# A second factor for GpSimd's softmax scalings, and plain copies where the factor is already in

## The chip, the cores and the metric

The kernel runs on one core of a Trainium2 chip. A core has five engines with instruction queues of their own, each worked off in order: TensorE (PE in the profile, its weight loads PEld) for matrix products and transposes, VectorE (DVE), ScalarE (ACT), GpSimd (POOL), and SyncE (SP), which here only issues DMAs. They wait for one another through semaphores. The metric is the device time of one execution in microseconds; before the change the median of three runs was 1030.27 us (1029.30 to 1031.94).

## The reference

Three stages follow one another, on float32 data. With B = 4 batches, H = 8 heads, S = 576 positions and D = 64:

```python
scores = q @ k.T / sqrt(D);  scores[causal] = -1e9
a = exp(scores - scores.max(-1));  a /= a.sum(-1) + 1e-9
local = a @ v
qp = phi(q)                                  # max(x, 0) + exp(min(x, 0))
mem_out = (qp @ M_prev) / (qp @ z_prev + 1e-6)
g = 1 / (1 + exp(-beta))                     # one gate per head
x = g * mem_out + (1 - g) * local            # 2304 tokens x 512
x = (h - tanh(h)) @ w_out,  h = x @ w_in     # first MoE layer, 512 -> 2048 -> 512
out = P(h) / (Q(h) + 1e-6) @ w2_out,  h = x @ w2_in   # second layer, a rational gate
```

So every row of the softmax is multiplied by two numbers before its product with v: one over its sum, which differs from row to row, and 1 - g, which is one number per head.

## The kernel before

Attention works on 16 head pairs n (4 batches x 4 pairs, two heads e = 0, 1 each). A head's 576 queries are cut into four rows of tiles i = 0 to 3 of 128 queries, which see (i + 1) x 128 keys, and a short tile i = 4 of 64 queries; the short tiles of both heads lie one above the other in one tile of 128 partitions, `p4`. For each (i, e): `scores` (TensorE) puts q k into a PSUM bank, `least` (VectorE) adds the mask and finds the extreme, `expo` (ScalarE) takes the exponential into the SBUF tile `p` with its row sums, `recip` (VectorE) makes one over the sum in `sm`, and `scale` (L919) multiplies `p` by it. Then `turn` (L941, TensorE) transposes `p` in blocks of 128 into a PSUM bank, `turned` (L956, ScalarE) copies the bank to the SBUF tile `pT`, and `values` (TensorE) forms the product with v. Each `p` tag has two buffers (`N_P`), `pT` has six.

Which engine scales is in `SCALES`, read at 2i + e: P is GpSimd, A is ScalarE, V is VectorE. That gives (0,0) P, (0,1) A, (1,0) V, (1,1) P, (2,0) P, (2,1) A, (3,0) P, (3,1) P and the short tile P; only for the first pair does VectorE scale (3,0). The gate factor 1 - g lies in the tile `omg`, one column for each head, made in `setup2`. It enters at one of two places. For rows 1 and the short tile it is the second factor of `scale` (L926, L929). For rows in `LATE` (0, 2, 3) `scale` multiplies by one over the sum alone (L931 on ScalarE, L933 on GpSimd or VectorE), and the copy in `turned` multiplies by `omg` (L966); the other copies are plain (L970). A copy empties a bank that holds one entry of `TURNS`: (2,0) with (0,0); (2,1) with (0,1); (3,0); (3,1); (1,0) with (1,1); and two for the short tile.

The order of all this is written out by hand: the tables `AT` and `OVER` give every step of every pair a virtual time (100 for a pair), and a heap issues the steps in that order, so that several pairs are in flight. From a virtual time of 842 on, `bg.tick` puts steps of the decoding of the first layer's weights between them (ScalarE L587 and L610, VectorE L589 to L598, GpSimd L612). Two chains of matrix products follow attention, with weights split into a high and a low part, in a fixed order too.

Of the kernel before, what the change touches and what calls it, by code (L numbers as in the profile page):

```python
# [10 lines left out]
F32 = mybir.dt.float32  # L11
# [4 lines left out]
ALU = mybir.AluOpType  # L16
# [3 lines left out]
P = 128  # L20
# [12 lines left out]
MIX = False  # L33
PSUM_DECODE = True
SCALES = "PAVPPAPPP"
LATE = (0, 2, 3)
LOW_ATT, LOW_POST, LOW_X = "P", "P", "P"
AGE_A, AGE_B, AGE_C = 1, 3, 4
EVERY = 3
TICKS_1 = (2, 2, 2, 3, 2, 3, 2, 2, 2, 2, 2, 0)  # L40
# [437 lines left out]
def kernel(  # L478
# [21 lines left out]
    nc = tc.nc  # L500
# [220 lines left out]
    class Attention:  # L721
# [197 lines left out]
        def scale(self, n, i, e):  # L919
            v, h = self.u[n, i], 2 * (n % NP)  # L920
            pt, r = v["p"][e], v["sm"][:, 6 + e:7 + e]
            how = "V" if (n, i, e) == (0, NQ - 1, 0) else SCALES[2 * i + e]
            eng = nc.vector if how == "V" else nc.gpsimd
            if i == NQ:
                og = self.cp["omg4"][:, n % NP:n % NP + 1]
                eng.tensor_scalar(pt[:, 0:S], pt[:, 0:S], r, og, ALU.mult, ALU.mult)  # L926
            elif i not in LATE:
                og = self.cp["omg"][:, h + e:h + e + 1]
                eng.tensor_scalar(pt, pt, r, og, ALU.mult, ALU.mult)  # L929
            elif how == "A":  # L930
                nc.scalar.activation(pt, pt, AF.Copy, scale=r)  # L931
            else:
                eng.tensor_scalar(pt, pt, r, None, ALU.mult)  # L933

        def busy(self, ps, count):

# [19 lines left out]
        def turned(self, n, k):  # L956
            ps = self.pair[n].pop(("tp", k))
            w = sum(nb for _, _, nb in TURNS[k])
            if w == 1:
                t = self.sp.tile([P, 1, P], F32, tag="pT5", name=f"pT{n}_{k}")  # L960
            else:
                t = self.sp.tile([P, NQ, P], F32, tag="pT", name=f"pT{n}_{k}", bufs=N_PT)
            dst, (i, e, _) = t[:, 0:w, :].rearrange("r t c -> r (t c)"), TURNS[k][0]
            if i in LATE:
                c = 2 * (n % NP) + e
                nc.scalar.activation(  # L966
                    dst, ps[:, 0:w * P], AF.Copy, scale=self.cp["omg"][:, c:c + 1]
                )
            else:
                nc.scalar.copy(dst, ps[:, 0:w * P])  # L970
            c = 0
            for i, e, nb in TURNS[k]:
                self.u[n, i].setdefault("pT", {})[e] = t[:, c:c + nb]
                c += nb
# [73 lines left out]
        def start(self, setup):  # L1048

            self.load_k(-1)  # L1050
            setup()
            self.load("qn", 0, [P, NQ + 1, P], qn, 2)
            self.load_v(0)
            self.load_z(0)
            self.load_tails()
# [216 lines left out]
    cpool = att.enter_context(tc.tile_pool(name="ac", bufs=1, side="right"))  # L1272
    sp = att.enter_context(tc.tile_pool(name="as", bufs=2, side="right"))
    cp = {}
# [3 lines left out]
    cp["g"] = cpool.tile([P, H], F32, tag="gg", name="gg")  # L1278
    cp["omg"] = cpool.tile([P, H], F32, tag="omg", name="omg")
    cp["omg4"] = cpool.tile([P, NP], F32, tag="omg4", name="omg4")  # L1280
    cp["g4"] = cpool.tile([P, NP], F32, tag="g4", name="g4")
    cp["sm"] = [cpool.tile([P, 8], F32, tag=f"sm{j}", name=f"sm{j}") for j in range(2 * NQ + 2)]
    cp["rq"] = [cpool.tile([P, S + TAIL], F32, tag=f"rq{j}", name=f"rq{j}") for j in range(2)]
# [7 lines left out]
    def setup():  # L1291
        attn.load_q(-1)
        nc.vector.memset(cp["idle"], 0.0)
        attn.busy(bT("idle"), IDLE)
        for t in cp["rq"]:
            nc.vector.memset(t[0:D, TAIL:P], 0.0)
            nc.vector.memset(t[D:P, 0:TAIL], 0.0)
        nc.gpsimd.memset(cp["mask"], 0.0)
        nc.gpsimd.affine_select(
            out=cp["mask"][:, TB:TB + P], in_=cp["mask"][:, TB:TB + P],  # L1300
            compare_op=ALU.is_ge, fill=NEG, base=0, pattern=[[-1, P]],
            channel_multiplier=1,
        )
        make_identity(nc, cp["ident"])
        for e in range(2):
            r = slice(e * TAIL, (e + 1) * TAIL)
            nc.vector.tensor_copy(cp["mask4"][r], cp["mask"][0:TAIL, TB:TB + TAIL])
        for m in cp["mb"]:
            nc.vector.memset(m, 0.0)
        nc.vector.memset(cp["p4"][:, S:S + TAIL], 0.0)  # L1310
        for sm in cp["sm"]:
            nc.vector.memset(sm, 1e-9)
        for pz in cp["pz"]:
            nc.vector.memset(pz[:, :, :, D:D + 1], 1e-6)

# [16 lines left out]
    one = Moe1(xs_a, range(NT // TA), TA, FA, wka, bHa, bYa, False, nc.vector)  # L1332
# [31 lines left out]
    for f in FB[len(FB) - KEEP:]:  # L1364
        bg.add(1, f, w_keep)
    attn.start(setup)
    calls, events = attn.events(), []
    rows = range(B * NP)
# [21 lines left out]
    while events:  # L1390
        at, _, name, n = heapq.heappop(events)
# [211 lines left out]
```

## Time and profile before

| | |
|---|---|
| median of three runs | 1030.27 us |
| the profiled execution | 1033.54 us |
| its span, first to last instruction | 1031.4 us |
| TensorE, VectorE, ScalarE, GpSimd busy in the span | 98%, 75%, 70%, 36% |
| mean granted TensorE clock | 0.992 of full speed |
| attention | about 7 to 212 us |
| first MoE layer | about 212 to 622 us |
| second MoE layer | about 622 to 1031 us |

The shares are means over stages of different kinds. In slices of a fortieth of the span, ScalarE is busy nine tenths or more in most of the first eight (attention) and seven tenths or less in the ten from the eleventh on, and GpSimd is busy eight to nine tenths in several of the first eight and a few tenths after them. Matrix products are pipelined, and the profile models their ends. Records on one engine overlap by up to 0.1 us, so that durations read one by one add up to slightly more than the time they fill.

### The profile page before, as it was taken

The numbers are of one execution on the slowest core, as the hardware profiler recorded it, in microseconds if no ns is written. First come the engines' busy times: TensorE is split into PE (matmuls) and PEld (weight loads), VectorE is DVE, ScalarE is ACT, GpSimd is POOL, SyncE is SP. The second block draws the span as 40 slices with busy tenths as digits, with TensorE's granted clock in tenths as the row PEclk, the third lists the DMA queues.
The fourth block names the chain that finished last, engine by engine and source line by source line (L and its number), as shares of the span: only waits on it lengthen the run. The fifth ranks groups of instructions, "written<-read, shape, count | busy, mean of one in ns | idle before, by whom it ended". The sixth has DMA issues, their size and how long they took to land.

```text
span 1031.4 us, 17897 instructions
## 1 busy us (share of the span) xinstructions
PE 1006.1 (98%) x6446; PEld 910.5 (88%) x6446; DVE 775.1 (75%) x1755; ACT 720.3 (70%) x1524; POOL 370.0 (36%) x338
## 2 busy tenths in 40 slices
PE   7989999989999999999999999999999999999998
PEld 4767766779998999999999998999999999999997
DVE  6768899878887367676665657987887877877885
ACT  5979999946765333333333547988888888888886
POOL 3878899924553010000000102342332423324221
PEclk8999999999999999999999999999999999999999
DMA  4434555243332125353534241000000000000000
GB/s 116 120 111 116 186 155 154 94 115 119 117 103 82 42 69 153 116 154 92 153 99 146 97 135 36 21 1 32 1 11 21 1 31 1 1 31 1 25 7 31
DMA packets 36376, 79.81 MB, mean 77 GB/s; under 512 B 8384, under 2 KB 10944, under 8 KB 36288
## 3 DMA queue, kind: packets, MB, share of 16 engines
q1 hardware_dynamic: 35824, 78.40, 25.1%
q8 instruction: 51, 0.84, 0.3%
q10 hardware_dynamic: 464, 0.27, 0.1%
q14 instruction: 37, 0.30, 0.1%
HBM read 64.49 MB, written 14.16 MB: 76 GB/s over the span
## 4 chain that ended last, share of the span: by engine, by line
PE 85%; DVE 6%; POOL 5%; ACT 2%; issue 1%; DMA 0%; ACTq 0%; POOLq 0%; DVEq 0%
PE h L1081 37%; PE y L1211 19%; PE y L1128 19%; PE pv L1006 3%; POOL p L933 2%; PE s L876 2%; PE tp L950 2%; DVE p L892 2%; PE pv L990 1%; POOL p L929 1%; POOL p L926 1%; ACT p L905 1%; DVE x L1265 1%; PE pw L1006 0%; PE php L838 0%
## 5 line engine op out<-in xcount | busy, mean ns | idle before, releaser
L1081 PE MATMUL h<-xs,w 128*128 128x384 f32 (+1 forms) x2448 | 436.4, 327 | 1.0 <-DVE g L1193 0.6
L1081 PEld LDWEIGHTS h<-xs,w 128*128 128x128 f32 x2448 | 409.6, 189 | 10.3 <-DVE g L1193 1.1
L1128 PE MATMUL y<-gh,w 128*128 128x384 f32 (+1 forms) x864 | 215.9, 318 | 2.1 <-ACT gh L1116 2.1
L1211 PE MATMUL y<-w,gh 128*128 128x512 f32 x576 | 179.6, 393 | 0.0
L1128 PEld LDWEIGHTS y<-gh,w 128*128 128x128 f32 x864 | 152.7, 189 | 2.6 <-ACT gh L1116 2.3
L1073 POOL TENSOR_TENSOR xs<-x,xs 128x256 fp32r<-128x256 f32 (+1 forms) x56 | 46.1, 849 | 274.0 <-ACT xs L1072 250.6
L1128 PE MATMUL y<-gl,w 128*128 128x384 f32 (+1 forms) x432 | 137.8, 319 | 3.4 <-DVE gl L1117 3.2
L1110 ACT ACTIVATE g<-h 128x384 f32<-128x384 f32 (+1 forms) x108 | 49.2, 455 | 127.9 <-PE h L1081 122.0
L1111 DVE TENSOR_TENSOR g<-h,g 128x384 f32<-128x384 f32 (+1 forms) x108 | 55.2, 511 | 91.8 <-ACT g L1110 91.6
L1211 PEld LDWEIGHTS y<-w,gh 128*128 128x128 f32 x576 | 106.8, 188 | 17.4
L1211 PE MATMUL y<-w,gl 128*128 128x512 f32 x288 | 114.0, 396 | 0.2
L1200 POOL TENSOR_TENSOR gl<-g,gh 128x384 fp32r<-128x384 f32 x48 | 49.5, 1031 | 150.2 <-ACT gh L1198 150.2
L1200 POOL TENSOR_TENSOR gl<-vG,gh 128x384 fp32r<-128x384 f32 x47 | 50.2, 1068 | 130.9 <-ACT gh L1198 128.7
L1116 ACT CAST gh<-g 128x384 fp32r<-128x384 f32 (+1 forms) x108 | 51.3, 475 | 62.6 <-PE y L1128 60.0
L905 ACT ACTIVATE p<-p,sm 128x128 f32<-128x128 f32 (+4 forms) x144 | 84.1, 590 | 7.7 <-DVE sm L892 6.6
L933 POOL TENSOR_SCALAR p<-p,sm 128x512 f32<-128x512 f32 (+2 forms) x63 | 80.2, 1282 | 20.1 <-DVE gg L1319 11.8
L1187 DVE TENSOR_TENSOR vA<-vA,vC 128x384 f32<-128x384 f32 x96 | 53.5, 557 | 43.0 <-ACT vC L1181 43.0
L1128 PEld LDWEIGHTS y<-gl,w 128*128 128x128 f32 x432 | 81.8, 189 | 4.1 <-DVE gl L1117 4.0
L1117 DVE TENSOR_TENSOR gl<-g,gh 128x384 fp32r<-128x384 f32 (+1 forms) x108 | 63.2, 585 | 29.5 <-ACT gh L1116 29.5
L892 DVE CUSTOM_DVE_ANT_0 p<-s,mask 128x512 f32<-128x512 f32 (+4 forms) x160 | 69.5, 477 | 14.4 <-PE s L876 13.1
L1176 DVE SCALAR_TENSOR_TENSOR vA<-vA,vC 128x384 f32<-128x384 f32 x96 | 59.1, 616 | 25.3 <-ACT vC L1175 20.2
L1180 ACT ACTIVATE vA<-h 128x384 f32<-128x384 f32 x96 | 46.9, 489 | 39.4 <-PE h L1081 37.4
(110 smaller groups left out, 1685.7 us busy)
## 6 DMA issues: line engine op xcount, KB each, us to landing
wraw<-in_w_in_dram SPq DMA_DIRECT2D x32, 512.0 KB, 4.0
wraw<-in_w_out_dram SPq DMA_DIRECT2D x32, 512.0 KB, 4.0
wk<-wf SPq DMA_DIRECT2D x36, 256.0 KB, 4.3
wx<-wk SPq DMA_DIRECT2D x18, 512.0 KB, 3.3
qn<-in_qn_dram SPq DMA_DIRECT2D x16, 320.0 KB, 3.8
vn<-in_vn_dram SPq DMA_DIRECT2D x16, 320.0 KB, 3.3
out_dram<-o SPq DMA_DIRECT2D x18, 256.0 KB, 2.0
rk<-in_kd_dram SPq DMA_DIRECT2D x30, 144.0 KB, 2.9
```

The costliest lines, as they stand in the source:

```text
L892: nc.vector.tensor_tensor_reduce(out=v["p"][-1][:, k0:k1], in0=bank[:, c0:c0 + k1 - k0], in1=mask, scale=-0.125, scalar=3.0e38, op0=ALU.ad ...
L905: nc.scalar.activation(pt, pt, AF.Exp, bias=sm[:, c:c + 1], scale=-1.0, accum_out=sm[:, 2 * e:2 * e + 1],)
L933: eng.tensor_scalar(pt, pt, r, None, ALU.mult)
L1081: nc.tensor.matmul(ps[:, 0:T], wi_of(layer, f, wp, k), xs[k][:, xp], start=(n == 0), stop=(n == 3 * NK - 1),)
L1111: nc.vector.tensor_tensor(v["g"], v["h"], v["g"], ALU.subtract)
L1116: nc.scalar.copy(v["gh"], v["g"])
L1117: self.lo.tensor_tensor(v["gl"], v["g"], v["gh"].bitcast(F32), ALU.subtract)
L1128: nc.tensor.matmul(ps, wo_of(1, f, w)[:, m * P:(m + 1) * P], v[g], start=(first and j == 0 and m % n == 0), stop=(last and j == 2), skip_g ...
L1176: nc.vector.scalar_tensor_tensor(A, A, QEPS, C, ALU.add, ALU.mult)
L1187: nc.vector.tensor_tensor(n["A"], n["A"], n["C"], ALU.mult)
L1200: eng.tensor_tensor(o["gl"], o["G"], o["gh"].bitcast(F32), ALU.subtract)
L1211: nc.tensor.matmul(acc_of[t][m], g[:, c], wo_of(2, f, w), start=(first and j == 0), stop=(last and j == 2),)
```

## The change

`LATE` now holds pairs (i, e), and only the two that ScalarE scales: (0,1) and (2,1). In `scale`, GpSimd and VectorE always multiply by two factors in one instruction, one over the sum and the gate factor; for an (i, e) in `LATE` that they would scale the second factor would be a column of ones, `one`, a new tile that set-up fills. In `turned`, the copy multiplies by the gate factor only if the first entry of the bank is in `LATE`. The tables of the order stay as they are.

```diff
-LATE = (0, 2, 3)
+LATE = ((0, 1), (2, 1))
...
             if i == NQ:
                 og = self.cp["omg4"][:, n % NP:n % NP + 1]
                 eng.tensor_scalar(pt[:, 0:S], pt[:, 0:S], r, og, ALU.mult, ALU.mult)
-            elif i not in LATE:
-                og = self.cp["omg"][:, h + e:h + e + 1]
-                eng.tensor_scalar(pt, pt, r, og, ALU.mult, ALU.mult)
             elif how == "A":
                 nc.scalar.activation(pt, pt, AF.Copy, scale=r)
             else:
-                eng.tensor_scalar(pt, pt, r, None, ALU.mult)
+                og = self.cp["one"] if (i, e) in LATE else self.cp["omg"][:, h + e:h + e + 1]
+                eng.tensor_scalar(pt, pt, r, og, ALU.mult, ALU.mult)
...
-            if i in LATE:
+            if (i, e) in LATE:
                 c = 2 * (n % NP) + e
...
+    cp["one"] = cpool.tile([P, 1], F32, tag="one", name="one")
...
+        nc.vector.memset(cp["one"], 1.0)
```

## Rows read from the trace of the kernel before

**Rows 1.** The page, part 1: busy us (share of the span) xinstructions

```profile
PE 1006.1 (98%) x6446; PEld 910.5 (88%) x6446; DVE 775.1 (75%) x1755; ACT 720.3 (70%) x1524; POOL 370.0 (36%) x338
```

**Rows 2.** Windows; columns as in the first line

```profile
core 0: us, PE busy (x) PEld busy (x) DVE busy (x) ACT busy (x) POOL busy (x), PEclk, DMA share, GB/s
91.50:102.77 11.27, 11.27 (x116) 8.51 (x118) 9.12 (x39) 10.83 (x31) 9.73 (x9) 1.00 0.41 119
114.04:125.77 11.73, 11.70 (x117) 8.54 (x118) 10.99 (x41) 11.73 (x34) 8.67 (x9) 1.00 0.30 91
150.77:163.10 12.33, 11.49 (x116) 8.48 (x118) 11.45 (x45) 12.05 (x33) 12.33 (x10) 1.00 0.52 158
125.77:199.58 73.81, 67.88 (x678) 50.25 (x680) 68.65 (x247) 72.19 (x193) 73.81 (x55) 1.00 0.47 142
440.00:624.00 184.00, 184.00 (x1063) 184.00 (x1062) 117.93 (x207) 75.85 (x151) 16.58 (x16) 1.00 0.42 125
```

**Rows 3.** Chain of waits, 150 to 163 us: start us, us, what

```profile
156.05 2.07 POOL p L933 x2
158.12 1.35 POOL p L926
159.47 1.63 POOL p L929
```

**Rows 4.** TensorE in order of time: start, us, instruction [idle before <-releaser]

```profile
53.14 0.76 PE L950 MATMUL tp<-ident,p 128*128 128x128 f32 x5 [0.95 <-POOL p L933]
54.68 0.65 PE L950 MATMUL tp<-ident,p 128*128 128x128 f32 x4 [0.78 <-POOL p L933]
...
71.42 0.66 PE L950 MATMUL tp<-ident,p 128*128 128x128 f32 x4 [0.89 <-POOL p L933]
```

**Rows 5.** Windows after the stall at 53 to 55 us (columns of rows 2)

```profile
55.00:57.00 2.00, 2.00 (x8) 0.54 (x5) 0.83 (x1) 0.44 (x1) 1.67 (x2) 0.59 0.30 88
57.00:59.00 2.00, 2.00 (x22) 1.79 (x21) 1.76 (x7) 0.00 (x0) 1.26 (x1) 0.56 0.00 0
```

**Rows 6.** GpSimd in order of time, both forms of the scaling, undisturbed

```profile
46.07 0.55 POOL L929 TENSOR_SCALAR p<-p,sm,omg 128x256 f32<-128x256 f32 x1
47.95 0.82 POOL L926 TENSOR_SCALAR p<-p,sm,omg 128x576 f32<-128x576 f32 x1 [1.33 <-DVE sm L914]
...
69.80 1.57 POOL L933 TENSOR_SCALAR p<-p,sm 128x512 f32<-128x512 f32 x1
...
72.56 0.61 POOL L933 TENSOR_SCALAR p<-p,sm 128x128 f32<-128x128 f32 x1
74.35 1.25 POOL L933 TENSOR_SCALAR p<-p,sm 128x384 f32<-128x384 f32 x1 [1.18 <-DVE sm L914]
```

**Rows 7.** GpSimd's groups by shape, 140 to 200 us: busy us, mean ns

```profile
L929 POOL TENSOR_SCALAR p<-p,sm,omg 128x256 f32<-128x256 f32 x5 | 7.5, 1498 | 0.0
...
L926 POOL TENSOR_SCALAR p<-p,sm,omg 128x576 f32<-128x576 f32 x5 | 6.9, 1388 | 0.0
```

**Rows 8.** ScalarE's groups by shape, whole span

```profile
L966 ACT ACTIVATE pT<-tp,omg 128x512 f32<-128x512 f32 x64 | 42.4, 690 | 7.9 <-PE tp L950 4.2 <-PE pv L1006 3.7
L970 ACT COPY pT<-tp 128x512 f32<-128x512 f32 x32 | 18.6, 584 | 1.1 <-PE tp L950 1.0
```

**Rows 9.** VectorE and GpSimd in order of time, first pair

```profile
14.18 0.45 DVE L1321 TENSOR_SCALAR omg<-gg 128x8 f32<-128x8 f32 x1
...
14.02 1.24 POOL L933 TENSOR_SCALAR p<-p,sm 128x384 f32<-128x384 f32 x1 [11.79 <-DVE gg L1319]
18.07 0.70 POOL L929 TENSOR_SCALAR p<-p,sm,omg 128x256 f32<-128x256 f32 x1 [2.80 <-DVE sm L917]
```

**Rows 10.** VectorE in order of time, a pair that GpSimd bounds

```profile
158.19 0.67 DVE L594 SCALAR_TENSOR_TENSOR wf<-wraw,wf 128x512 uint32<-128x512 uint32 x1
158.89 1.12 DVE L598 SCALAR_TENSOR_TENSOR wf<-wraw,wf 128x512 uint32<-128x512 uint32 x1
159.93 0.81 DVE L807 SCALAR_TENSOR_TENSOR phi<-qn,phi 128x640 f32<-128x640 f32 x1
```

**Rows 11.** GpSimd's groups by shape, 20 to 80 us

```profile
L929 POOL TENSOR_SCALAR p<-p,sm,omg 128x256 f32<-128x256 f32 x4 | 2.3, 577 | 0.0
```

## The prediction

> **What bounds the kernel now.** I read the busy table first: TensorE is busy 1006.1 of 1031.4 us and GpSimd only 370.0 [rows 1], so an edit of GpSimd looks worthless until the span is cut into stages. From about 232 us on, the kernel is matrix products almost back to back; from 440 to 624 us TensorE is busy all of 184.00 us [rows 2]. Nothing that this change touches runs there, so whatever attention (the first 210 us) gains should be carried to the end.
>
> The second view is a table of windows, cut where the value products of successive head pairs begin [rows 2]. Three kinds of pair are seen. At 91 to 103 us a pair takes 11.27 us, and TensorE is busy for all of it. At 114 to 126 us, where weight decoding joins in, it takes 11.73 us, and ScalarE is busy for all of it. In the six pairs from 125.77 to 199.58 us GpSimd is busy for all of 73.81 us; the one shown takes 12.33 us, of which TensorE works 11.49 and ScalarE 12.05. So GpSimd is the bound of six pairs, by 0.3 us a pair over ScalarE and 0.8 us over TensorE.
>
> Third, the chain of waits inside that pair [rows 3]: two one-factor scalings, the two-factor scaling of the short tile, then the two-factor one of row 1 on GpSimd, for which TensorE waits. Fourth, TensorE's waits before 80 us [rows 4]: transposes wait for one-factor scalings at 53.14 (0.95 us), 54.68 (0.78) and 71.42 (0.89). [...]
>
> **The change, part by part.**
>
> *GpSimd's scalings.* By the code each of the 16 pairs has four one-factor scalings on GpSimd (two of 512 columns, one of 384, one of 128) but for one that the first pair gives to VectorE: 63. Each gets a second factor. Undisturbed, one-factor rows last 1.57, 1.25 and 0.61 us for 512, 384 and 128 columns, and two-factor rows 0.82 us for 576 and 0.55 us for 256 [rows 6]: the form with more work is the shorter one. Two-factor is a line of (0.82 - 0.55) / (576 - 256) = 0.84 ns a column plus 0.33 us; one-factor one of (1.57 - 0.61) / 384 = 2.5 ns plus 0.29 us. By the first line the changed scalings would last 0.77, 0.66 and 0.44 us, an estimate, since these widths have no two-factor row: a pair's four fall from 2 x 1.57 + 1.25 + 0.61 = 5.0 us to 2 x 0.77 + 0.66 + 0.44 = 2.6 us. The other end: in the bound pairs the two-factor rows are stretched to means of 1.39 us (576) and 1.50 us (256) [rows 7], by 0.57 and 0.95 us. All four stretched by 0.95 us would make 6.4 us, dearer than now. I take 2.6 to 3.6 us, nearest the undisturbed rows, because what stretches them is limited (first rival). Even 3.6 us takes GpSimd's pair from 12.33 to 10.9 us, below the other two engines.
>
> [...]
>
> *ScalarE's copies.* Of a pair's four scaled 512-column copies, three become plain. Scaled they last 690 ns, plain 584 [rows 8]: 0.11 us each, 0.32 us a pair. The fourth keeps its factor, since ScalarE still does the one-factor scalings (0,1) and (2,1). The new tile of ones is read by nobody, because every pair in LATE is scaled by ScalarE, ahead of that branch; its memset is one small VectorE instruction among the set-up's, before the first scores are there: nothing.
>
> *The new wait.* In the first pair the scaling at 14.02 us must now wait for the gate factor, ready at 14.18 + 0.45 us [rows 9]. Behind it on GpSimd is the row-1 scaling, which starts only at 18.07 us after 2.80 us of idle: a delay of some 0.8 us, less 0.6 us of shortening, is hidden. Without that cover it would cost 0.2 us once. In later pairs the factor has long been there. VectorE's one changed instruction keeps its engine and width and is taken at nothing. No DMA and no queue order changes.
>
> **The sum.** Before 80 us the waits at 53, 55 and 71 us go, 0.95 + 0.78 + 0.89 = 2.6 us: the two 512-column scalings ahead of each last transpose are together 1.6 us shorter. ScalarE does not take over there; it works 0.44 of the 4 us after the stall [rows 5]. With the double stall gone the clock should stay up: 2 x 0.41 + 2 x 0.44 = 1.7 us [rows 5]; a pair that leaves TensorE idle for 12.33 - 11.49 = 0.84 us still has a clock of 1.00 [rows 2], so a small rest would not lower it. Small gains before 50 us: 0.2. Together 4.5 us, with ends 1.7 (one stall left, clock falling as before) and 5.2.
>
> From 114 to 200 us ScalarE is late next. Its work is 11.73 + 72.19 = 83.9 us [rows 2], less 7 x 0.32 = 81.7; with TensorE's 11.70 in the first of the seven windows 82.0. They last 11.73 + 73.81 = 85.5 us now. Closed up entirely, 3.5 us are gained; I leave 0.1 us of idle in each of five pairs: 3.0. Ends: 1.5 (a pair's 0.3 us of ScalarE idle stays) and 3.8.
>
> From 91 to 114 us nothing, since TensorE is full. Last pair and hand-over to the first MoE layer: 0.2, the three cheaper copies.
>
> 4.5 + 3.0 + 0.2 = 7.7 us. The profiled execution took 1033.54 us (span 1031.4), 3.3 us above the median of the runs, 1030.27; so 1025.8 by it, and 1022.6 us as the runs are timed.
>
> **Rivals.**
>
> *Contention makes it slower.* The short, dense two-factor form could be the one that collides with VectorE: the row-1 scaling lasts 1.63 us in the bound pair [rows 3] against 0.55 alone, and beside it one of VectorE's weight steps lasts 1.12 us, where its twin before it took 0.67 [rows 10]. If each of the four new ones caught that 1.08 us, they would hold 2.6 + 4.3 = 6.9 us instead of the bound pair's 2 x 1.57 + 2.07 = 5.2; 12.33 would become 14.0, and six pairs would cost 10 us: with nothing gained earlier, about 1040. It decides at 0.65 us of stretch each. Against it: before 80 us the row-1 scaling has a mean of 577 ns [rows 11]; and in the bound pair the partners are VectorE's three instructions that read two tiles, 0.67 + 0.67 + 0.81 = 2.2 us undisturbed, of which 0.54 + 1.08 = 1.6 us already fall on the two existing two-factor scalings.
>
> [...]
>
> *The form does not matter.* If the slow rows are slow for another reason (their buffers, what runs beside them), GpSimd keeps its time, only ScalarE's 0.32 us a pair is saved, and ScalarE is off the bound in six pairs of seven: 0 to 0.7 us, about 1029.8. Against it: the rows of each form lie on a line in columns, and row 1's buffers are of the same pool as the others'.
>
> *GpSimd gains, but the next wait eats part.* TensorE, ScalarE and VectorE in their fixed orders hold one another: the bound pairs fall only to about 12.1 us, 1.3 us in all, and before 80 us the stalls go but the clock still falls. 2.6 + 1.3 = 3.9 us, 1026.4. For it: ScalarE already works 98% of those pairs [rows 2].
>
> **How the numbers follow.** Forecast, 1020.3 to 1025.5: 0.62. The next wait eats part, 1025 to 1028: 0.24. The form does not matter: 0.09. Contention: 0.05. With the scatter of the runs (1029.30 to 1031.94) the range is 1019.0 to 1027.8. A measurement of this kernel can tell 0.3%, 3.1 us, from no change. The first two cases are faster by more than that, but for a corner of the second (0.02): faster 0.84, within 0.3% 0.11, slower 0.05.
>
> **What would show it.** 512-column scalings near 0.8 us in the early pairs; TensorE without the waits at 53, 55 and 71 us, and a clock of 1.0 after them; 11.8 to 11.9 us for the pairs that took 12.33, with ScalarE full in place of GpSimd; plain copies at 0.58 us. The prediction is wrong if the changed 512-column scalings stay above 1.4 us, if those pairs stay at 12.3 us, or if the stages after 232 us change their length.

## The result, and the profile after

The median fell from 1030.72 us (4 runs) to 1020.25 us (4 runs, 1019.75 to 1020.97): 10.5 us, a ratio of 0.9899 with a 95% interval of 0.9882 to 0.9917. Forecast were 7.7 us less and 1022.6 us, with a range of 1019.0 to 1027.8; the time lies near the lower end of the range, at the very edge of the first case (1020.3 to 1025.5). The profiled execution took 1020.13 us, its span is 1017.9 us. It is 13.4 us below that of before, more than the medians are apart; a likely reason is told further down.

GpSimd's scalings as groups over the whole span, of which [rows 6] showed single instructions. L931 is now the line of all but the short tile's. Columns: busy us, mean ns | idle before and releaser.

```profile
L931 POOL TENSOR_SCALAR p<-p,sm,omg 128x512 f32<-128x512 f32 x31 | 23.9, 779 | 9.4 <-DVE sm L917 9.2 <-DVE x L1263 0.2
L926 POOL TENSOR_SCALAR p<-p,sm,omg 128x576 f32<-128x576 f32 x16 | 13.9, 870 | 3.9 <-PE php L838 2.2 <-DVE sm L914 1.7
L931 POOL TENSOR_SCALAR p<-p,sm,omg 128x384 f32<-128x384 f32 x16 | 11.1, 696 | 22.4 <-ACT p L905 13.7 <-DVE sm L914 6.0 <-ACT pT L968 1.8
L931 POOL TENSOR_SCALAR p<-p,sm,omg 128x256 f32<-128x256 f32 x16 | 10.3, 642 | 3.7 <-DVE sm L917 3.7
L931 POOL TENSOR_SCALAR p<-p,sm,omg 128x128 f32<-128x128 f32 x16 | 8.5, 531 | 0.5 <-DVE sm L914 0.5
```

512 columns now take half of the 1.57 us of [rows 6], near the 0.77 of the estimate; 384 columns, at 696 ns, are close to their 0.66, and 128 columns, at 531 ns, lie a fifth above their 0.44. The two scalings that were not edited shrank too, from 1154 to 870 ns (576 columns) and from 1054 to 642 ns (256) as means of all 16.

The windows that answer to [rows 2], and one over 50 to 59 us for [rows 5]; the columns are in the first line, here and for the windows of all experiments below:

```profile
core 0: us, PE busy (x) PEld busy (x) DVE busy (x) ACT busy (x) POOL busy (x), PEclk, DMA share, GB/s
85.29:96.56 11.27, 11.27 (x116) 8.52 (x118) 8.87 (x39) 10.63 (x31) 6.80 (x9) 1.00 0.38 118
142.33:153.87 11.54, 11.49 (x116) 8.50 (x118) 10.97 (x43) 11.54 (x34) 8.02 (x10) 1.00 0.54 161
119.24:187.99 68.75, 68.28 (x679) 50.34 (x680) 65.74 (x244) 68.75 (x193) 49.50 (x54) 1.00 0.50 149
440.00:624.00 184.00, 183.97 (x1058) 183.31 (x1058) 118.45 (x208) 79.47 (x155) 17.93 (x17) 1.00 0.38 115
...
50.00:59.00 9.00, 9.00 (x94) 6.50 (x94) 7.78 (x33) 8.66 (x26) 6.04 (x7) 1.00 0.40 113
```

The six pairs that GpSimd bounded take 68.75 us instead of 73.81. One takes 11.54 us; ScalarE is busy for all of it, GpSimd for 8.02. Pairs that TensorE bounds still take 11.27 us. From 50 to 59 us TensorE does not idle and the clock is 1.00.

TensorE's waits from 20 to 200 us (us in total, times, longest), in the kernel before and then after the change. Before, ten were for a scaling: four for one with one factor (three of them in [rows 4]) and six for row 1 in the bound pairs. None is left.

```profile
PE tp L950 <- POOL p L929: 5.9, 6, 1.4
PE tp L950 <- POOL p L933: 3.3, 4, 0.9
```
```profile
PE pw L988 <- DVE x L1263: 0.9, 1, 0.9
PE s L876 <- DVE sm L892: 0.2, 1, 0.2
PE php L838 <- ACT pT L968: 0.2, 1, 0.2
```

GpSimd in the pair at 142 us, and VectorE's three two-tile instructions after it, as in [rows 3] and [rows 10]:

```profile
147.68 0.82 POOL L926 TENSOR_SCALAR p<-p,sm,omg 128x576 f32<-128x576 f32 x1
148.48 0.72 POOL L931 TENSOR_SCALAR p<-p,sm,omg 128x256 f32<-128x256 f32 x1
```
```profile
149.72 0.68 DVE L594 SCALAR_TENSOR_TENSOR wf<-wraw,wf 128x512 uint32<-128x512 uint32 x1
150.44 0.69 DVE L598 SCALAR_TENSOR_TENSOR wf<-wraw,wf 128x512 uint32<-128x512 uint32 x1
151.05 0.82 DVE L807 SCALAR_TENSOR_TENSOR phi<-qn,phi 128x640 f32<-128x640 f32 x1
```

Before, these two scalings ran at the same time as VectorE's three and lasted 1.35 and 1.63 us; now GpSimd reaches them earlier, is done at 149.2 us, and the three start at 149.72.

### The profile page after: what moved, and what is told of

Read it like the earlier page. It is cut to its first block, busy times and chain, and to the rows that moved or that the text cites. A ratio compares the mean times of both kernels' runs of the same rounds, so it can differ in the third digit from the quotient of the medians.

```text
span 1017.9 us, 17898 instructions
## 1 busy us (share of the span) xinstructions
PE 1002.1 (98%) x6446; PEld 908.7 (89%) x6446; DVE 770.3 (76%) x1756; ACT 714.6 (70%) x1524; POOL 321.2 (32%) x338
## 4 chain that ended last, share of the span: by engine, by line
PE 88%; ACT 8%; DVE 3%; issue 1%; DMA 0%; POOL 0%; ACTq 0%; DVEq 0%
PE h L1079 38%; PE y L1209 19%; PE y L1126 19%; PE s L876 4%; ACT p L905 3%; PE tp L948 3%; PE pv L1004 2%; ACT pT L968 2%; PE pv L988 1%; PE pw L1004 1%; PE php L838 1%; DVE p L892 1%; ACT p L928 0%; ACT phiT L845 0%; ACT wf L587 0%
## 5 line engine op out<-in xcount | busy, mean ns | idle before, releaser
L905 ACT ACTIVATE p<-p,sm 128x128 f32<-128x128 f32 (+4 forms) x144 | 87.5, 623 | 6.9 <-DVE sm L892 5.8
L876 PE MATMUL s<-rk,rq 64*128 64x384 f32 (+5 forms) x320 | 67.3, 467 | 3.1 <-DMA rq<-in_qd_dram 2.6
```

The costliest lines, as they stand in the source:

```text
L876: nc.tensor.matmul(bank[:, c0:c0 + k1 - k0], d["rq"][r, q0:q0 + P], d["rk"][r, k0:k1], start=True, stop=True, skip_group_check=True,)
L905: nc.scalar.activation(pt, pt, AF.Exp, bias=sm[:, c:c + 1], scale=-1.0, accum_out=sm[:, 2 * e:2 * e + 1],)
```

## The experiments

Each time is a median of several runs, beside runs of the kernel before on the same chip, unless it says otherwise; a ratio is to the kernel before. The edits shown are made to the changed kernel, but for that of the plain copies alone, which is made to the kernel before.

**The form alone.** The second factor is the column of ones, the copies keep the gate factor.

```diff
-LATE = ((0, 1), (2, 1))
+LATE = ((0, 0), (0, 1), (2, 0), (2, 1), (3, 0), (3, 1))
```

> Two factors in all of GpSimd's scalings, the second one a column of ones; the four ScalarE copies of a pair keep their gate factor as before. Theory (the form of GpSimd's scalings carries the gain): the pairs that took 12.33 us fall to 11.54 + 0.32 = 11.86 us at most, so about 8 of the 10.5 us are kept: 1022 to 1023.5 us. Rival (ScalarE's cheaper copies carry it, since ScalarE is full after the change): at most half is kept, 1025.5 us or more.

1023.08 us, ratio 0.9921 (0.9908 to 0.9934). The multiplication by one changes no value, and it brings nearly four fifths of the gain. A window over one of the bound pairs:

```profile
142.87:154.69 11.82, 11.68 (x116) 8.50 (x118) 11.06 (x43) 11.82 (x35) 8.12 (x10) 1.00 0.54 165
```

**The plain copies alone.**

```diff
-            if i in LATE:
+            if (i, e) in ((0, 1), (2, 1)):
```

> Three of the four ScalarE copies of a pair are plain, GpSimd's scalings keep one factor; the gate factor of rows (0,0), (2,0), (3,0) and (3,1) is left out of the computation. Theory (form of GpSimd's scalings): GpSimd still bounds six pairs at 12.3 us, so 0 to 1 us is gained: 1029.7 to 1030.7 us. Rival (ScalarE's copies): 5 us or more, 1025.5 us or less.

1031.24 us, against 1031.13 for the kernel before in the same runs, ratio 1.0001 (0.9990 to 1.0012): nothing. In the windows of its trace GpSimd's pair is 12.33 us as before, while ScalarE's busy time fell from 12.05 to 11.76:

```profile
149.15:161.48 12.33, 11.49 (x116) 8.49 (x118) 11.45 (x45) 11.76 (x33) 12.33 (x10) 1.00 0.51 153
54.00:58.00 4.00, 3.24 (x38) 2.32 (x40) 2.11 (x8) 1.91 (x5) 3.25 (x4) 1.00 0.44 117
```

The second line matters for the clock. In this execution TensorE's two waits near 53 us are there nearly as in [rows 4] (0.76 and 0.77 us for 0.95 and 0.78), and the clock is 1.00 after them, where [rows 5] had 0.59 and 0.56.

**Only the 512-column scalings.** As the form alone, but rows 0 and 2 keep one factor.

```diff
+                if i in (0, 2):
+                    eng.tensor_scalar(pt, pt, r, None, ALU.mult)
+                else:
+                    eng.tensor_scalar(pt, pt, r, og, ALU.mult, ALU.mult)
```

> As the run with ones, but the second factor only in the two 512-column scalings of a pair; those of 384 and 128 columns keep one factor. Theory (GpSimd only has to fall below ScalarE): GpSimd's pair falls by 1.6 us to about 10.7, below ScalarE's 11.86, and the early waits were behind 512-column scalings, so the time is within 1.5 us of the run with ones: 1022 to 1025 us. Rival (every us of GpSimd counts, by its latency in the chain): only 3.2 of GpSimd's 5.2 us are treated, so about 60% of the gain of the run with ones: 1025 to 1027 us.

1024.63 us, ratio 0.9936 (0.9923 to 0.9948), 1.55 us above the form alone, against 1.5 as the theory's limit and 2 to 4 for the rival: inside the theory's 1022 to 1025 us, if barely. A bound pair takes 11.81 us (window below) with GpSimd busy for 9.53: there the remaining one-factor scalings, 1273 and 767 ns on average, cost nothing. From the third pair on, the pairs are as long as with ones throughout. What the trace shows as lost is early and small: the value products of the third pair begin at 54.6 us instead of 52.6, and the distance stays 2.0 us from there on, but 1.2 of these were there before any scaling, since VectorE's first score came at 9.66 instead of 8.45 us. Where the rest of the 1.55 us between the medians comes from is not shown.

```profile
144.93:156.74 11.81, 11.67 (x116) 8.52 (x118) 11.44 (x43) 11.81 (x34) 9.53 (x10) 1.00 0.51 159
```

**An immediate as the second factor** (one run). `LATE` is that of the form alone.

```diff
-                og = self.cp["one"] if (i, e) in LATE else ...
+                og = 1.0 if (i, e) in LATE else ...
```

> The run with ones, but the second factor of GpSimd's 512-, 384- and 128-column scalings is an immediate 1.0 in place of a column. Theory (a second operation selects the fast form, whatever feeds it): 512 columns stay at about 0.77 us, time about 1023 us. Rival (it takes a second operand from a column to be fast): 512 columns take 1.5 us as with one factor, and the time is about 1030 us.

1023.79 us, and GpSimd's groups over the whole span:

```profile
L931 POOL TENSOR_SCALAR p<-p,sm 128x512 f32<-128x512 f32 x31 | 21.5, 704 | 10.2 <-DVE sm L917 7.0 <-ACT pT L964 2.7 <-DVE x L1263 0.5
...
L931 POOL TENSOR_SCALAR p<-p,sm 128x384 f32<-128x384 f32 x16 | 9.9, 622 | 26.8 <-DVE sm L914 14.8 <-DVE gg L1319 12.0
L931 POOL TENSOR_SCALAR p<-p,sm 128x128 f32<-128x128 f32 x16 | 6.7, 418 | 0.6 <-DVE sm L914 0.6
```

No second column is read, and 512 columns take 704 ns, against 1574 with one factor in the kernel before and 770 with the column of ones (means of 31 each). In these traces two operations took less time than one, with a column or an immediate as the second factor.

**ScalarE's two scalings moved to GpSimd as well.**

```diff
-SCALES = "PAVPPAPPP"
-LATE = ((0, 1), (2, 1))
+SCALES = "PPVPPPPPP"
+LATE = ()
```

> The change, and besides the one-factor scalings (0,1) and (2,1) move from ScalarE to GpSimd with two factors, so that all copies are plain. Theory (after the change ScalarE is the bound of seven pairs, GpSimd has 3.5 us a pair to spare, TensorE's floor is 11.27): ScalarE loses about 0.9 us a pair, GpSimd gains 1.1, the pairs fall from 11.54 to 11.27 to 11.4 us: 1 to 2 us faster than the change, 1018 to 1019.5 us. Rival (TensorE and VectorE in their order hold the pair at 11.54 already, ScalarE only looks full): no gain, 1020.3 us, or a loss where GpSimd gets in VectorE's way.

1025.59 us, ratio 0.9945 (0.9933 to 0.9958): 5 us slower than the change. The theory missed; the rival's last clause, a loss where GpSimd gets in VectorE's way, is what came in the pairs from 122 us on. These took 12.00 us, and no engine is full in them; the chain of waits runs through VectorE from 113 us on. Here are GpSimd and VectorE in order of time, and the window of that pair:

```profile
149.57 1.27 POOL L828 TENSOR_TENSOR phi<-phi,nrm 128x640 f32<-128x640 f32 x1
150.81 0.69 POOL L931 TENSOR_SCALAR p<-p,sm,omg 128x128 f32<-128x128 f32 x1
```
```profile
149.94 1.24 DVE L799 TENSOR_SCALAR phi<-qn 128x640 f32<-128x640 f32 x1
```
```profile
146.12:158.12 12.00, 11.53 (x116) 8.54 (x118) 11.68 (x45) 11.07 (x31) 9.60 (x12) 1.00 0.51 150
```

VectorE's L799, which follows the masking of row 1, lasts 1.24 us here; its median is 0.49 us in the kernel before and 0.50 in the change. It starts 0.37 us into GpSimd's L828 and ends 0.3 us after that is through (149.94 + 1.24 = 151.18 against 150.84). The added 384-column scaling, 0.67 us long, stands ahead of L828 on GpSimd and pushed it onto L799; in the change's pair at 142 us L828 is through at 144.57 + 1.26 = 145.83 and L799 starts at 146.02. In the kernel before the order was the other one: L799 began 0.11 us ahead of L828 and kept its 0.49 us, while L828 lasted 1.50 us, against 1.27 above:

```profile
166.79 0.49 DVE L799 TENSOR_SCALAR phi<-qn 128x640 f32<-128x640 f32 x1
```
```profile
166.90 1.50 POOL L828 TENSOR_TENSOR phi<-phi,nrm 128x640 f32<-128x640 f32 x1
```

In both the instruction that started second lasted longer than it does elsewhere. What held it is in no row.

This is about half of the loss. From VectorE's first score to the value products of the eighth pair the run took 101.6 us against 98.8 in the change, so 2.8 us were gone before any L799 lasted this long: there TensorE waits for GpSimd itself, 0.65 us for a scaling at 41.85 us and 1.17 us for L828 at 59.91.

**ScalarE's two scalings left out.** GpSimd's and VectorE's work as in the change.

```diff
-                nc.scalar.activation(pt, pt, AF.Copy, scale=r)
+                pass
...
-            if (i, e) in LATE:
+            if False:
```

> The change, with ScalarE's scalings of (0,1) and (2,1) left out and their copies plain, so both factors of those two rows are missing from the computation; GpSimd and VectorE do what they do in the change. ScalarE loses about 0.9 us a pair. Theory (after the change ScalarE bounds the pair of 11.54 us; moving these scalings to GpSimd failed because GpSimd then blocked VectorE): TensorE becomes the bound, 11.27 to 11.35 us a pair, 1.3 to 2 us less than the change: 1018.2 to 1019 us. Rival (TensorE and VectorE in their order hold the pair at 11.54 themselves): the pair stays at 11.5 us and the time at 1020 us.

1018.63 us, ratio 0.9881 (0.9867 to 0.9894), and pairs of 11.27 us that TensorE fills. So ScalarE does bound the pair of 11.54 us, and the room for a gain was there: in the late pairs the move to GpSimd ended at 12.00 us, with VectorE's L799 at 1.24 us beside L828. The window of a pair:

```profile
142.38:153.65 11.27, 11.27 (x117) 8.51 (x118) 10.91 (x43) 10.90 (x30) 8.41 (x10) 1.00 0.53 160
```

**One scaling moved, of 128 or of 384 columns.**

```diff
-SCALES = "PAVPPAPPP"
+SCALES = "PPVPPAPPP"    # or "PAVPPPPPP"
```

> The change, and the 128-column scaling (0,1) moves from ScalarE to GpSimd, with the column of ones as its second factor; the copy of its bank keeps the gate factor. ScalarE's pair falls by 0.29 to 11.25 us, GpSimd's rises by 0.45. Theory (ScalarE bounds): pairs of 11.3 to 11.4 us if GpSimd's addition meets none of VectorE's instructions, 1 to 1.7 us less than the change, 1018.5 to 1019.3 us; as slow as the run with both moved, 12.0 us a pair, if the addition meets VectorE. Rival (TensorE and VectorE hold the pair): 1020.3 us at best.

> The change, and only the 384-column scaling (2,1) moves from ScalarE to GpSimd, with the column of ones; copies as in the change. ScalarE's pair falls by 0.51 to 11.03 us, GpSimd's rises by 0.66. Theory as for the 128-column one: 11.3 us a pair, 1018.3 to 1019 us, if it meets none of VectorE's instructions. This scaling came right behind the plane product on GpSimd in the run with both moved and was not stretched there, so of the two single moves this one should be the better. Rival: 1020.3 us at best.

128 columns: 1021.25 us, 0.9905 (0.9890 to 0.9920), not to be told from the change. Its bound pairs fell to 11.36 us as expected, but the first pairs lost that again: TensorE waits 0.69 us for GpSimd's L828 at 57.89 us, and one early pair takes 10.49 us instead of 9.58. 384 columns: 1023.30 us, 0.9929 (0.9916 to 0.9941), slower than the change; the pairs take 11.88 us. I had taken it for the better of the two, and it is the worse: it is the one that stands ahead of L828, and VectorE's L799 again begins 0.37 us into L828, lasts 1.25 us and ends 0.36 us after it (GpSimd, then VectorE, in order of time):

```profile
147.29 1.26 POOL L828 TENSOR_TENSOR phi<-phi,nrm 128x640 f32<-128x640 f32 x1
```
```profile
147.66 1.25 DVE L799 TENSOR_SCALAR phi<-qn 128x640 f32<-128x640 f32 x1
```

**128 columns moved in the later pairs only, beside the change again.**

```diff
+            if n >= 7 and (i, e) == (0, 1):
+                how = "P"
```

> The change, and the 128-column scaling (0,1) moves from ScalarE to GpSimd only in pairs 7 to 15, where ScalarE bounds; the first seven pairs stay as in the change, since the run that moved it everywhere lost about 1 us before 65 us. Theory: pairs of 11.37 instead of 11.54 us in seven windows and the start of the change: about 1.2 us less than the change, 1018.8 to 1019.4 us. Rival (the loss of the full move sits in the late pairs or behind them): no better than the change.

> The change itself, on the same chip as the run beside it: 1020.3 us, and by a second profile whether windows of 11.54 us with ScalarE full, and no TensorE wait at 53, 55 and 71 us, come again.

1020.77 us (0.9897, 0.9879 to 0.9916) against 1021.37 us for the change (0.9901, 0.9883 to 0.9919). The 0.6 us between them is inside what the runs scatter (1020.56 to 1021.65 and 1019.72 to 1022.43); an advantage over the change is not shown. The early pairs were as in the change and the later ones took 11.37 us. The second profile of the change again has pairs of 11.54 to 11.56 us and no TensorE wait for a scaling.

## Why the prediction was right, and where it was off

**GpSimd's scalings** were the cause, and the two-factor line gave their size: 0.77 us estimated for 512 columns, 779 ns measured. The ones (1023.08 us against 1031.13 before, 770 ns for 512 columns) and the immediate (704 ns) show that it was the second operation, and no other thing, that was behind it. I had the changed scalings at 2.6 to 3.6 us a pair; four of them take 2 x 0.77 + 0.66 + 0.53 = 2.7 us at 140 to 200 us. Not foreseen was that the 576- and 256-column ones would get cheaper by 1.4 us a pair (1.35 + 1.63 to 0.82 + 0.72): GpSimd is done with them at 149.20 us, 0.52 us before VectorE's three instructions begin, beside which they had run before. That did not matter for the time, since GpSimd was already below the others.

**114 to 200 us: 3.0 us forecast, 5.4 measured** (85.5 to 80.2 us between the same value products, at 107.8 and 187.9 us after). This is the term that was mis-sized most, and it even exceeds its upper end of 3.8. The engine that is late next was right, ScalarE, shown by leaving its work out; its floor was not. I took it from busy time, 12.05 us of a pair. Here is ScalarE before the change, in order of time, over a stretch of the bound pairs:

```profile
160.91 0.70 ACT L966 ACTIVATE pT<-tp,omg 128x512 f32<-128x512 f32 x1
161.62 0.59 ACT L970 COPY pT<-tp 128x512 f32<-128x512 f32 x1
...
167.14 0.22 ACT L905 ACTIVATION_READ_ACCUMULATOR p<-p,sm 128x1 f32 x1
167.61 1.27 ACT L966 ACTIVATE pT<-tp,omg 128x512 f32<-128x512 f32 x2 [0.25 <-PE tp L950]
```

From one start to the next the copy holds the engine 161.62 - 160.91 = 0.71 us, and the scaled copy at 157.55 us 0.57; the read of the accumulator 0.47 us, where others take 0.09. So 0.14 + 0.38 = 0.52 us of a pair's 12.33 were waiting, of which the trace names 0.25. ScalarE's work by starts was 12.33 - 0.52 = 11.81 us, which is the pair of 11.82 us that the form alone left. Less three copies at 0.57 - 0.47 = 0.10 us that makes 11.5, and the change has 11.54. The copies' own term was right: in the seven windows the change is 82.1 - 80.2 = 1.9 us shorter than the form alone (2.8 us between the two medians), 7 x 0.32 = 2.2 forecast. It can be seen in starts alone. As a duration the plain copy did not show the 0.58 us that I had named as a sign: its mean is 619 ns, and in the bound pairs the records of ScalarE overlap more than before, the untouched 512-column exponential with a mean of 829 ns where it had 721, while its starts are 0.62 us apart in both.

**Before 80 us: 4.5 us forecast, 3.4 to 4.2 measured, none of it by the clock.** The waits at 53, 55 and 71 us went, as predicted. But the fall of the clock need not have come. With nearly the same waits the run with plain copies kept it at 1.00; whether 0.2 us less of waiting or chance made this difference is not shown. The two profiles of the change show that one kernel can do either. At the end of attention TensorE waits 2.71 us for VectorE in both; from 208 to 212 us the clock is then 1.00 in the first profile and 0.62 in the second:

```profile
207.32 0.38 PE L1126 MATMUL y<-gl,w 128*128 128x256 f32 x1 [2.71 <-DVE gl L1115]
208.00:212.00 4.00, 4.00 (x37) 4.00 (x36) 2.82 (x6) 2.43 (x8) 1.91 (x3) 1.00 0.90 245
```
```profile
207.89 0.39 PE L1126 MATMUL y<-gl,w 128*128 128x256 f32 x1 [2.71 <-DVE gl L1115]
208.00:212.00 4.00, 4.00 (x23) 4.00 (x24) 3.11 (x6) 1.65 (x5) 0.79 (x2) 0.62 0.77 210
```

The profiled execution of the kernel before was one of its longer ones (1033.54 us; the median was 1030.72), and it had the fall after this same wait too, 0.50 from 219.4 to 222.0 us, that the first profile of the change did not have. These two falls, 1.7 and about 1.4 us, would account for the profiles being 13.4 us apart and the medians 10.5.

Without the clock I had 2.8 us. Measured against the run with plain copies, from the first score on VectorE to the value products of the fifth pair, it is 69.2 - 65.0 = 4.2 us. The second profile of the change has 65.8 us there, so 3.4 us gained: in it a score product at 45.12 us took 1.93 us where the first has 1.14, and no row names what held it. Of the 4.2 us, 0.8 came before the first value products: before the change transposes waited there for a 512-column scaling. The prediction names no wait ahead of 53 us, and had 0.2 for all of that time.

```profile
23.30 0.66 PE L950 MATMUL tp<-ident,p 128*128 128x128 f32 x4 [0.72 <-POOL p L933]
```

**The sum.** 4.2 + 5.4 + 0.5 (last pair, 8.2 to 7.7 us; 0.2 forecast) = 10.1 us, near the 10.5 of the medians; with the second profile's early pairs it is 9.2, and the rest is not located. The forecast of 7.7 was 6.0 us of gain where it happens and 1.7 us of clock that one execution had and another need not: two errors that partly cancelled, so that the number came out nearer than its terms by luck.

**The new wait** was hidden: the first 384-column scaling started at 14.36 instead of 14.02 us and the row-1 scaling at 17.80. **The later stages** kept their length: 440 to 624 us is full of matrix products as before.

**The rivals.** That the form does not matter is refuted by the ones (1023.08 us against 1031.13). That the next wait eats part is refuted for the bound pairs; they fell further than forecast. Contention did not decide the change: a pair's four scalings took 2.7 us at 140 to 200 us, near the undisturbed end of the estimate. But at just this place some instructions lasted longer beside one of the other engine: before the change GpSimd's row-1 scaling, 1.63 us against 0.55 alone, and in the run with both scalings moved VectorE's L799, 1.24 us against 0.50. The limit on the stretch in the prediction counts only VectorE's three instructions that read two tiles; that only such instructions matter is not shown, and L799 reads one. That run is 5 us slower than the change, about half of it by this.

## What to carry to other kernels

Where an engine seems to be off the bound by its share of the span, cut the span into periods; a stage in which it is busy all the time can hide behind a mean of 36%, as GpSimd's 73.81 us without a rest did here. Take the floor of the next engine from the distance between starts of its instructions, not from its busy time, which here held half a microsecond of waits in 12. A fall of the clock in one profile is worth a look at a second execution before it enters a sum; and work moved to GpSimd is priced by whom it delays, here VectorE (L799 from 0.50 to 1.24 us) and TensorE (a wait of 1.17 us), and not by its own duration alone.

## What the runs showed of the hardware

- GpSimd's tensor_scalar from and to float32 in SBUF with one operation took 2.5 ns a column plus 0.29 us, with two (the second one a column) 0.84 ns plus 0.33, each a line through two undisturbed rows of the kernel before; at 512 columns 1.57 us before and 0.77 after were measured. Here a multiplication by 1.0 was worth adding: 1023.08 us against 1031.13.
- The immediate was the cheaper second operand, by much the same at each width, in one trace each: 704 against 770 ns (mean of 31 each) for 512 columns, 622 against 696 for 384, 418 against 492 for 128.
- A VectorE tensor_scalar over 640 columns that began 0.4 us into a GpSimd tensor_tensor lasted 1.24 us instead of a median of 0.50, until shortly after that one was through; where it began 0.11 us ahead, it took 0.49 us and the tensor_tensor 1.50 instead of 1.27.
- After the same TensorE wait of 2.71 us one execution of the change went on at a clock of 1.00 and another at 0.62 for 4 us. Two waits of 0.76 and 0.77 us near 53 us left the clock at 1.00 in one execution of a nearly equal kernel; 0.95 and 0.78 us in another were followed by 0.59 and 0.56.
